# Agent attention with a cosine feed-forward layer: the running maximum and sum of the keys made on GpSimd from copies in SBUF

## The chip, the cores and the metric

The kernel runs on one core of one Trainium2 chip. The metric is the device time of one execution in microseconds (us), the median over repeated runs. A core has five engines with queues of their own: PE (TensorE, matmuls; PEld is its weight load), DVE (VectorE), ACT (ScalarE), POOL (GpSimd) and SP (SyncE, which here only issues DMAs).

## What is computed

Four batches of 12480 queries, keys and values of width 128, with 49 agents per batch, go through agent attention; its output goes through a layer of 2048 hidden units whose activation is h·cos(h).

```python
def sm(a, b):
    s = scale * (a @ b.transpose(0, 2, 1))
    s = s - s.max(-1, keepdims=True)
    e = np.exp(s)
    return e / (e.sum(-1, keepdims=True) + 1e-09)
agent_v = sm(agents, k) @ v          # agents over all keys
x = sm(q, agents) @ agent_v          # queries over the 49 agents
h = x @ w_in
out = (h * np.cos(h)) @ w_out
```

## The kernel before

Names: batch b is 0 to 3; NG = 13 groups of 960 queries per batch; a group is worked in STEP = 16 steps, and a batch in PER = 208 steps. One **step** of the main loop (first_product, cubic_part, second_product) is: two matmuls of 480 columns into a tile `ph` (L1063), a Sin activation on ACT that reads `ph` and writes `c` (L1066), one SCALAR_TENSOR_TENSOR on DVE that makes r = (c - 1)·h from `c` in SBUF and `ph` in PSUM (L1072), and, four steps later, two matmuls of `r` (L1088). There are 832 steps, and three `ph` tiles, so PE can be at most three steps ahead of DVE. Every eight steps two more matmuls end an output chunk (L1084, L1085), and ACT copies it to SBUF (L1095).

Everything else is fitted between the steps of the batch before it, by a table of step numbers (`plan`, `extra`, `spread_out`, `burst`, `fill`). For batch b = 1 to 3 that is, in the steps of batch b - 1:

- **The scores of the keys** (`Later.scores`, g = 0 to 12, NL = 13): 64 small matmuls (L552) into a PSUM tile `one`, of which there are two; ACT copies it to `s` in SBUF (L556; for g = 0 to 2 of batch 1 DVE copies). For g > 0 DVE takes the running maximum `run` = max(`run`, scores) at L559, elementwise, 128x392 elements (96x98 for g = 12), from PSUM, or from `s` where DVE copied. The scores of a query group (L169, copy L689, row maximum L693 on DVE, subtraction L695 on POOL) lie between them.
- **The maximum** over all keys: `top` (L566), two small matmuls (L570, L578), and `shift`: POOL subtracts it from the thirteen parts of `s` (L584).
- **A burst** at step 97 of the batch: the exponentials of `s` (L587) and of two pieces of queries (L746).
- **The sums**: POOL adds the parts of exp(s) into `es` (L593, at steps 44 + 3g behind the burst) and sums each query's 49 weights by a tree of additions (`query_sum`, L757 to L761). `query_inverse` adds EPS = 1e-9 on DVE (L765) and takes the reciprocal (L766), over a whole piece of 5 to 7 groups. `inverse` first calls `total`, which reduces `es` on DVE (L611), copies the result (L612), and is followed by a matmul with ones (L617).
- **The values**: matmuls L516 and a DVE addition into `av` (L606).
- **The weights of the queries**: for each group POOL multiplies (L771) into one of two tiles `p`, PE transposes it six steps before the group's first step (L785), ACT copies (L790), and POOL splits the copy into a rounded part and a rest, `pT` (two CASTs L795, two subtractions L796). The products L1063 of the group read `pT`.

The order on an engine is that of a scheduler; what stands inside `kept_behind` is held behind what the named engine was given before it, and all that `plan` runs is so held on DVE. In the windows around the bursts the order on PE, DVE and ACT is as written.

Of the kernel before, what the change touches and what calls it, by code (L numbers as in the profile page):

```python
# [9 lines left out]
F32 = mybir.dt.float32  # L10
# [4 lines left out]
ALU = mybir.AluOpType  # L15
AX = mybir.AxisListType
PSUM = bass.MemoryType.PSUM

P = 128
# [9 lines left out]
EPS = 1e-9  # L29
# [9 lines left out]
HI = 64  # L39
# [7 lines left out]
def agent_attention_cos_ffn(ctx, tc, qT, kT, v, vk, vk_rest, agT, w_in, w_out, outT):  # L47
    nc = tc.nc
    NB, _, N = qT.shape
    NA = agT.shape[2]  # L50
    KR = HI + NA
# [204 lines left out]
    class Agents:  # L256
# [88 lines left out]
        def total(self):  # L345

            self.es2 = self.sb.tile([TT, KR], F32, name="es2", bufs=1)
            nc.gpsimd.memset(self.es2, 0.0)
            nc.vector.tensor_reduce(self.es2[:, :NA], self.es.rearrange("p t a -> p a t"), axis=AX.X, op=ALU.add)
            nc.vector.tensor_copy(self.es2[:, HI:], self.es2[:, :NA])  # L350
# [54 lines left out]
    NL = -(-N // FULL)  # L405
# [129 lines left out]
    class Later(First):  # L535

        def scores(self, g, by_vector=False):
            sb = self.sb
            if g == 0:
                self.s = sb.tile([P, NT_K, NA], F32, name="s", bufs=1)  # L540
                self.run = sb.tile([P, 8, NA], F32, name="run", bufs=1)
                self.es = sb.tile([P, 8, NA], F32, name="es", bufs=1)
                nc.gpsimd.memset(self.s[REST:, 8 * (NL - 1):], -1e30)
            n = min(FULL, N - g * FULL)
            xt = sb.tile([P, 2 * 512], F32, name="xt", bufs=3)[:, :n]
            load(xt, kT[self.b, :, g * FULL:g * FULL + n])
            s = self.part(g)
            w, k, _ = s.shape
            ps = self.psum()[:w, :k * NA].rearrange("p (t a) -> p t a", a=NA)
            for t in range(k):  # L550
                for j in range(w // QS):
                    mm = nc.tensor.matmul(ps[j * QS:(j + 1) * QS, t], xt[:, t * w + j * QS:t * w + (j + 1) * QS],  # L552
                                          ag[:, self.b, :], start=True, stop=True)
                    if t == j == 0:
                        behind(mm)
            (nc.vector.tensor_copy if by_vector else nc.scalar.copy)(s, ps)  # L556
            if g > 0:
                run = self.run[:w, :k]
                nc.vector.tensor_max(run, self.part(0) if g == 1 else run, s if by_vector else ps)  # L559

        def part(self, g):
            return self.s[:, 8 * g:8 * g + 8] if g + 1 < NL else self.s[:REST, 8 * g:]
# [43 lines left out]
                nc.vector.tensor_add(self.av[:, :NA], self.av[:, :NA], po)  # L606

        def total(self):
            self.es2 = self.sb.tile([P, KR], F32, name="es2", bufs=1)
            nc.gpsimd.memset(self.es2[:, NA:HI], 0.0)  # L610
            nc.vector.tensor_reduce(self.es2[:, :NA], self.es.rearrange("p t a -> p a t"), axis=AX.X, op=ALU.add)  # L611
            nc.vector.tensor_copy(self.es2[:, HI:], self.es2[:, :NA])  # L612

        def inverse(self):
            self.total()
            pa = self.psum()
            nc.tensor.matmul(pa[:KR, :1], self.es2, ones, start=True, stop=True)  # L617
            self.rz = self.sb.tile([KR, 1], F32, name="rz", bufs=1)
            nc.vector.tensor_scalar_add(self.rz, pa[:KR, :1], EPS)
            nc.vector.reciprocal(self.rz, self.rz)  # L620
# [14 lines left out]
    with ExitStack() as pools:  # L635
# [27 lines left out]
        PER = NG * STEP  # L663
        NQ = NB * NG
        NSTEP = NB * PER
        e_of, rz_of = {}, {}
        PIECES = 7

        def piece_tiles(piece):
            e = sb.tile([QT, PIECES * GT, NA], F32, name="e", bufs=3)  # L670
            rz = sb.tile([QT, PIECES * GT], F32, name="rz2", bufs=4)
            for i, k in enumerate(piece):
                e_of[k], rz_of[k] = e[:, i * GT:(i + 1) * GT], rz[:, i * GT:(i + 1) * GT]
                e_of[piece], rz_of[piece] = e[:, :len(piece) * GT], rz[:, :len(piece) * GT]

        def query_parts(n, piece, wide=False, by_vector=False):
            b, g = n // NG, n % NG
# [73 lines left out]
        def query_sum(n):  # L751

            e, rz = e_of[n], rz_of[n].unsqueeze(2)
            t = sb.tile([e.shape[0], GT, 24], F32, name="tree", bufs=1)
            src, w = e, 24
            while w > 2:
                nc.gpsimd.tensor_add(t[:, :, :w], src[:, :, :w], src[:, :, w:2 * w])  # L757
                src, w = t, w // 2
            nc.gpsimd.tensor_add(rz, t[:, :, 0:1], t[:, :, 1:2])
            nc.gpsimd.tensor_add(rz, rz, t[:, :, 2:3])  # L760
            nc.gpsimd.tensor_add(rz, rz, e[:, :, 48:49])  # L761

        def query_inverse(piece):
            rz = rz_of[piece]
            nc.vector.tensor_scalar_add(rz, rz, EPS)  # L765
            nc.vector.reciprocal(rz, rz)  # L766

        def query_weights(n):
# [226 lines left out]
        for b in range(1, NB):  # L995
            o, ps = (b - 1) * PER, pieces[b - 1]
            at = o + BURST
            qs = [x for piece in ps for x in scored(piece)][ahead:]
            ks = [(ab[b].scores, g) for g in range(3 if b == 1 else 0, NG)]
            before = sum(1 for x in qs) - AFTER  # L1000
            t = spread_out(mixed(ks, qs[:before]), t, at - TURN, True)
            t = extra(t, ab[b].across, dense=True)
            plan(t - 1, ab[b].top)
            t = extra(t + 1, ab[b].spread, dense=True) + 1
            for g in range(NL):
                plan(t + g, ab[b].shift, g)
            t = spread_out(qs[before:], t, at - 5, True)
            assert t < at, (t, at)
            work = dict(A=(query_exp, ps[0]), B=(query_exp, ps[1]), K=(pinned_exp, ab[b]))
            burst(at, [work[x] for x in ('A', 'K', 'B')])  # L1010
            fresh = scored(pieces[b][0], False, True)
            ahead = len(fresh)
            vs = [(ab[b].values, g) for g in range(NG)]
            judged(at)
            fill(at, fresh, vs)
            fresh = [x[:3] for x in fresh]
            for g in range(1, NL):
                plan(at + 44 + 3 * g, ab[b].add, g)
            t, end = at + 5, o + PER - 26
            todo = mixed(vs, fresh)  # L1020
            for i, x in enumerate(todo):
                t = extra(t, *x, dense=True) + 1
                if i + 1 < len(todo):
                    t += max(0, (end - t) // (len(todo) - i - 1) - 1)
            t = extra(t, ab[b].folded) + 1
            t = extra(t, ab[b].inverse) + 1
            i = b % 2
            for c in range(DFF // 512):
                t = extra(t, ab[b].project, c, a[i], dense=True) + 1
            t = extra(t, ab[b].project_out, wio, b1[i], b2[i], dense=True)  # L1030
            later.append((ab[b], a[i]))
            t += 1
            assert t < o + PER + 4, (t, o + PER)
# [256 lines left out]
```

## Time and profile before

| | |
|---|---|
| median of 3 runs | 1098.57 us (1098.48 to 1100.44) |
| the profiled execution's own time | 1100.26 us |
| its span, first to last instruction | 1098.5 us |
| what lies around the span | 1.8 us |
| PE busy | 1044.0 us (95%) |
| DVE busy | 1027.6 us (94%) |
| ACT busy | 954.1 us (87%) |
| POOL busy | 460.5 us (42%) |
| mean granted TensorE clock | 0.984 of full speed |

The profile is of one execution. Busy time is the time in which an engine had an instruction under way; matmuls are pipelined and their ends are modelled, so a busy PE is not PE at its peak. The waits name, for each idle stretch of an engine, the instruction whose end released it. The chain is followed back from the last instruction, at each step to what released it. L559 is line 559 of the kernel before; the changed file has other line numbers (L1072 becomes L1093).

### The profile page before, as it was taken

The page shows a single profiled execution, that of the slowest core. Times are in us where ns is not written, and L with a number is a line of the kernel's source. Part 1 is how long each engine was busy: PE and PEld are TensorE (multiplying, and loading weights), DVE is VectorE, ACT ScalarE, POOL GpSimd, SP SyncE. Part 2 cuts the span into 40 slices and gives each one's busy share as a digit, 9 for nine tenths or more (in the row PEclk, how much of TensorE's full clock was granted, in tenths as well). Part 3 has the DMA queues.
Part 4 walks back from the last instruction along what each step waited for, and adds up shares of the span by engine and source line. Part 5 has one row for each costly group of instructions (what it writes and reads, how often), then busy time and mean ns, then how long its engine had stood idle before and what let it go on. Part 6 is the DMA issues. An engine that isn't in the chain of part 4 may idle for free.

```text
span 1098.5 us, 28945 instructions
## 1 busy us (share of the span) xinstructions
PE 1044.0 (95%) x12029; PEld 797.2 (73%) x12029; DVE 1027.6 (94%) x1139; ACT 954.1 (87%) x1196; POOL 460.5 (42%) x761
## 2 busy tenths in 40 slices
PE   6888999799999999989999999989999999989997
PEld 2766777687877787677786788767776777767775
DVE  6879999699999999989998999979998999999997
ACT  4678888898989999899888999888888999999996
POOL 2432326784522223786543131678362312252220
PEclk9899999899999999999999999989999999989999
DMA  9933566522002245442111234441100000000001
GB/s 357 339 92 115 150 188 226 168 83 90 23 36 95 77 131 175 137 157 79 44 54 58 93 95 164 140 151 58 60 20 37 18 36 19 37 18 36 19 37 40
DMA packets 32557, 108.49 MB, mean 99 GB/s; under 512 B 3616, under 2 KB 4896, under 8 KB 32416
## 3 DMA queue, kind: packets, MB, share of 16 engines
q1 hardware_dynamic: 32416, 106.55, 29.0%
q8 instruction: 97, 1.59, 0.6%
q14 instruction: 44, 0.36, 0.1%
HBM read 80.97 MB, written 25.56 MB: 97 GB/s over the span
## 4 chain that ended last, share of the span: by engine, by line
PE 52%; DVE 29%; ACT 7%; POOL 6%; issue 4%; DMA 1%; SPq 0%; ACTq 0%; POOLq 0%; DVEq 0%
DVE r L1072 26%; PE ph L1063 21%; PE one L1088 18%; ACT c L1066 4%; POOL s L584 3%; PE one L516 3%; PE one L169 2%; PE one L1084 1%; PE one L552 1%; PE one L1085 1%; PE one L785 1%; ACT s L587 1%; PE one L373 1%; DVE run L559 1%; ACT osb L1095 1%
## 5 line engine op out<-in xcount | busy, mean ns | idle before, releaser
L1072 DVE SCALAR_TENSOR_TENSOR r<-c,ph 128x960 fp32r<-128x960 f32 x832 | 909.4, 1147 | 31.3 <-ACT c L1066 29.3
L1066 ACT ACTIVATE c<-ph 128x960 f32<-128x960 f32 x832 | 790.2, 979 | 99.4 <-PE ph L1063 75.7
L1063 PE MATMUL ph<-pT,a 113*128 113x480 f32 x1664 | 537.2, 403 | 18.2 <-DVE r L1072 11.8
L1088 PE MATMUL one<-r,w 128*128 128x480 f32 x1664 | 503.6, 389 | 0.4 <-DVE r L1072 0.4
L1063 PEld LDWEIGHTS ph<-pT,a 113*128 113x128 f32 x1664 | 287.7, 190 | 141.3 <-DVE r L1072 76.2
L1088 PEld LDWEIGHTS one<-r,w 128*128 128x128 f32 x1664 | 309.1, 190 | 50.8 <-DVE r L1072 1.4
L771 POOL TENSOR_TENSOR p<-e,rz 126x392 f32<-126x392 f32 (+1 forms) x52 | 44.2, 851 | 314.1 <-PE one L785 300.3
L796 POOL TENSOR_TENSOR pT<-p,pT 49x480 fp32r<-49x480 f32 x104 | 126.9, 1220 | 7.9
L795 POOL CAST pT<-p 49x480 fp32r<-49x480 f32 x104 | 60.7, 584 | 61.9 <-ACT p L790 57.5
L695 POOL TENSOR_TENSOR e<-e,mx 126x392 f32<-126x392 f32 x43 | 36.2, 842 | 90.4 <-DVE mx L693 90.0
L757 POOL TENSOR_TENSOR tree<-tree 126x96 f32<-126x96 f32 (+1 forms) x141 | 43.8, 311 | 10.6
L1095 ACT COPY osb<-one 128x480 f32<-128x480 f32 x80 | 44.5, 556 | 3.9 <-PE one L1088 3.9
L516 PEld LDWEIGHTS one<-s,vt 128*32 128x32 f32 (+1 forms) x2352 | 31.1, 115 | 22.6 <-issue 13.7
L516 PE MATMUL one<-s,vt 128*32 128x49 f32 (+1 forms) x2352 | 37.3, 216 | 10.2 <-ACT s L587 7.0
L169 PEld LDWEIGHTS one<-ag,xt 128*32 128x32 f32 (+1 forms) x2752 | 32.9, 109 | 17.4 <-issue 14.4
L169 PE MATMUL one<-ag,xt 128*32 128x49 f32 (+1 forms) x2752 | 39.1, 209 | 2.9 <-issue 2.9
L584 POOL TENSOR_TENSOR s<-s,mxb 128x392 f32<-128x392 f32 (+1 forms) x39 | 34.3, 911 | 17.1 <-DVE mxb L580 17.1
L1084 PE MATMUL one<-pT,b 113*128 113x480 f32 x104 | 40.5, 389 | 0.0
L1085 PE MATMUL one<-pT,b 113*128 113x480 f32 x104 | 40.0, 385 | 0.0
L552 PEld LDWEIGHTS one<-ag,xt 128*32 128x32 f32 x2340 | 28.3, 110 | 15.1 <-issue 7.7
L552 PE MATMUL one<-ag,xt 128*32 128x49 f32 x2340 | 33.6, 209 | 2.0 <-DVE s L556 2.0
L757 POOL TENSOR_TENSOR tree<-e 126x192 f32<-126x192 f32 (+1 forms) x47 | 28.9, 615 | 11.2 <-ACT e L746 8.9
(151 smaller groups left out, 654.9 us busy)
## 6 DMA issues: line engine op xcount, KB each, us to landing
xt<-qT SPq DMA_DIRECT2D x51, 480.0 KB, 4.0
outT<-osb SPq DMA_DIRECT2D x51, 480.0 KB, 2.7
xt<-kT SPq DMA_DIRECT2D x42, 512.0 KB, 3.8
vt<-vk SPq DMA_DIRECT2D x36, 512.0 KB, 4.5
c<-kT SPq DMA_DIRECT2D x6, 512.0 KB, 6.1
c<-vk SPq DMA_DIRECT2D x6, 512.0 KB, 7.4
xt<-vk SPq DMA_DIRECT2D x6, 512.0 KB, 7.6
vt<-w_in SPq DMA_DIRECT2D x8, 256.0 KB, 6.4
```

What stands on the lines that cost most here:

```text
L169: mm = nc.tensor.matmul(out[at:at + n], xt[:, t * TT + lo:t * TT + lo + n], ag, start=True, stop=True)
L516: mm = nc.tensor.matmul(po[rows], vt[:, x, rows], e, start=(first and x == 0), stop=(last and x + 1 == len(es)))
L552: mm = nc.tensor.matmul(ps[j * QS:(j + 1) * QS, t], xt[:, t * w + j * QS:t * w + (j + 1) * QS], ag[:, self.b, :], start=True, stop=True)
L584: nc.gpsimd.tensor_sub(s, s, self.mxb.unsqueeze(1).to_broadcast(list(s.shape)))
L757: nc.gpsimd.tensor_add(t[:, :, :w], src[:, :, :w], src[:, :, w:2 * w])
L795: nc.gpsimd.tensor_copy(pT[own, c], p[own])
L796: nc.gpsimd.tensor_sub(pT[other, c], p[own], pT[own, c].bitcast(F32))
L1063: nc.tensor.matmul(ph[:, j, :CH], ai[:, f], pTs[q % 3][:, c], start=True, stop=True)
L1066: nc.scalar.activation(cos, h, AF.Sin, bias=HALF_PI, scale=1.0)
L1072: nc.vector.scalar_tensor_tensor(r, cos, 1.0, h, op0=ALU.subtract, op1=ALU.mult)
L1088: nc.tensor.matmul(po, w1[:, f, :], r[:, j, :], start=(f == 0), stop=(f == NF - 1))
L1095: nc.scalar.copy(osb[:, c * CH:(c + 1) * CH], po)
```

## The change

For g = 1 to 10 of each of the batches 1 to 3 the running maximum is no longer one DVE instruction but three on POOL (`larger`): the difference y - x into a tile `over`, its maximum with 0, and x plus that; y is the copy `s` in SBUF. For g = 11 and 12 DVE takes the maximum, always from PSUM. `total` is made on POOL, by additions that halve `es` three times, and is planned 83 steps behind the burst, no longer called by `inverse`. The constant EPS of a piece of queries is added on POOL behind the sum of the piece's last group, for all pieces but the `early` one and the first three groups of the kernel.

```diff
@@ Later.scores
             if g > 0:
                 run = self.run[:w, :k]
-                nc.vector.tensor_max(run, self.part(0) if g == 1 else run, s if by_vector else ps)
+                old = self.part(0) if g == 1 else run
+                if g < NL - 2:
+                    self.larger(run, old, s)
+                else:
+                    nc.vector.tensor_max(run, old, ps)
+
+        def larger(self, out, x, y):
+
+            over = self.sb.tile([P, 8, NA], F32, name="over", bufs=1)
+            with kept_behind([nc.gpsimd.engine]):
+                nc.gpsimd.tensor_sub(over, y, x)
+                nc.gpsimd.tensor_scalar(over, over, 0.0, None, op0=ALU.max)
+                nc.gpsimd.tensor_add(out, x, over)
@@ Later.total, inverse
         def total(self):
+            es = self.es
             self.es2 = self.sb.tile([P, KR], F32, name="es2", bufs=1)
-            nc.gpsimd.memset(self.es2[:, NA:HI], 0.0)
-            nc.vector.tensor_reduce(self.es2[:, :NA], self.es.rearrange("p t a -> p a t"), axis=AX.X, op=ALU.add)
-            nc.vector.tensor_copy(self.es2[:, HI:], self.es2[:, :NA])
+            with kept_behind([nc.gpsimd.engine]):
+                nc.gpsimd.memset(self.es2[:, NA:HI], 0.0)
+                for n in (4, 2):
+                    nc.gpsimd.tensor_add(es[:, :n], es[:, :n], es[:, n:2 * n])
+                for x in (slice(0, NA), slice(HI, KR)):
+                    nc.gpsimd.tensor_add(self.es2[:, x], es[:, 0], es[:, 1])
 
         def inverse(self):
-            self.total()
@@ piece_tiles
+            if piece != early:
+                closes[piece[-1]] = piece
@@ query_sum, query_inverse
             nc.gpsimd.tensor_add(rz, rz, e[:, :, 48:49])
+            if n in closes:
+                nc.gpsimd.tensor_scalar_add(rz_of[closes[n]], rz_of[closes[n]], EPS)
 
         def query_inverse(piece):
             rz = rz_of[piece]
-            nc.vector.tensor_scalar_add(rz, rz, EPS)
+            if piece not in closes.values():
+                nc.vector.tensor_scalar_add(rz, rz, EPS)
             nc.vector.reciprocal(rz, rz)
@@ the plan of batch b
             for g in range(1, NL):
                 plan(at + 44 + 3 * g, ab[b].add, g)
+            plan(at + 44 + 3 * NL, ab[b].total)
```

How the instructions move, at three places. First DVE, where the keys of batch 2 are scored (`run` is the running maximum, `mx` the row maximum of a query group, `r<-c,ph` the steps). Before:

```order
L693 TENSOR_REDUCE mx_5004<-e 126x8
L1072 SCALAR_TENSOR_TENSOR r<-c,ph 128x960 x8
L559 TENSOR_TENSOR run<-s,one 128x392
L1072 SCALAR_TENSOR_TENSOR r<-c,ph 128x960 x8
L559 TENSOR_TENSOR run<-run,one 128x392
```

and in the change:

```order
L710 TENSOR_REDUCE mx_5036<-e 126x8
L1093 SCALAR_TENSOR_TENSOR r<-c,ph 128x960 x36
L710 TENSOR_REDUCE mx_5603<-e 126x8
L1093 SCALAR_TENSOR_TENSOR r<-c,ph 128x960 x28
L710 TENSOR_REDUCE mx_6098<-e 126x8
L1093 SCALAR_TENSOR_TENSOR r<-c,ph 128x960 x10
L563 TENSOR_TENSOR run<-run,one 128x392
```

The maxima between the steps are gone up to the eleventh, which stays on DVE.

Second POOL at the same place (`p` is the weights of a query group, `pT` its split copy). Before:

```order
L695 TENSOR_TENSOR e<-e,mx_5004 126x392
L771 TENSOR_TENSOR p_104<-e,rz_2366 126x2x4x49
L795 CAST pT_100<-p 49x480 x2
L796 TENSOR_TENSOR pT_100<-p,pT_100 49x480 x2
L771 TENSOR_TENSOR p_105<-e,rz_2366 126x2x4x49
L795 CAST pT_98<-p 49x480 x2
```

and in the change:

```order
L712 TENSOR_TENSOR e<-e,mx_5036 126x392
L569 TENSOR_TENSOR over<-s 128x392
L570 TENSOR_SCALAR over<-over 128x392
L571 TENSOR_TENSOR run<-s,over 128x392
L791 TENSOR_TENSOR p_104<-e,rz_2396 126x2x4x49
L815 CAST pT_100<-p 49x480 x2
L816 TENSOR_TENSOR pT_100<-p,pT_100 49x480 x2
L569 TENSOR_TENSOR over<-s,run 128x392
L570 TENSOR_SCALAR over<-over 128x392
L571 TENSOR_TENSOR run<-run,over 128x392
```

The three instructions stand between one group's `pT` and the next group's `p`, not between a `p` and its `pT`.

Third POOL in the denser scores of batch 1, where it is otherwise at one place. In the change:

```order
L569 TENSOR_TENSOR over<-s,run 128x392
L570 TENSOR_SCALAR over<-over 128x392
L791 TENSOR_TENSOR p_104<-e,rz_751 126x2x4x49
L571 TENSOR_TENSOR run<-run,over 128x392
L815 CAST pT_99<-p 49x480 x2
L816 TENSOR_TENSOR pT_99<-p,pT_99 49x480 x2
```

Here the last of the three comes between the weights `p` and the split copy `pT`.

## Rows read from the trace of the kernel before

**Rows 1.** The page's first part: busy us (share of the span) and instructions of each engine.
```profile
PE 1044.0 (95%) x12029; PEld 797.2 (73%) x12029; DVE 1027.6 (94%) x1139; ACT 954.1 (87%) x1196; POOL 460.5 (42%) x761
```
**Rows 2.** The page's chain that ended last, by line.
```profile
DVE r L1072 26%; PE ph L1063 21%; PE one L1088 18%; ACT c L1066 4%; POOL s L584 3%; PE one L516 3%; PE one L169 2%; PE one L1084 1%; PE one L552 1%; PE one L1085 1%; PE one L785 1%; ACT s L587 1%; PE one L373 1%; DVE run L559 1%; ACT osb L1095 1%
```
**Rows 3.** Busy time by stretch: length, each engine's busy us, clock, DMA share, GB/s.
```profile
105.00:175.00 70.00, 69.67 (x1460) 55.07 (x1458) 67.94 (x80) 60.43 (x81) 24.41 (x29) 1.00 0.58 177
345.00:387.00 42.00, 41.60 (x484) 32.34 (x484) 41.45 (x42) 38.25 (x49) 9.75 (x11) 1.00 0.27 86
387.00:436.00 49.00, 48.88 (x714) 39.46 (x713) 48.37 (x50) 44.85 (x59) 14.03 (x16) 1.00 0.44 139
...
180.00:250.00 70.00, 64.18 (x1056) 51.03 (x1056) 60.47 (x69) 62.01 (x67) 57.23 (x123) 0.95 0.40 129
850.00:950.00 100.00, 99.18 (x423) 72.87 (x421) 99.64 (x95) 94.26 (x120) 26.74 (x30) 1.00 0.06 25
```
**Rows 4.** The chain in order of time: start us, us on the chain, what.
```profile
99.09 0.57 DVE run L559
...
262.31 0.77 DVE rz L765
...
321.18 0.76 DVE es L611
...
657.74 0.47 DVE run L559
```
**Rows 5.** Groups by line and shape: count, busy us, mean ns, idle before, releasers.
```profile
L1072 DVE SCALAR_TENSOR_TENSOR r<-c,ph 128x960 fp32r<-128x960 f32 x832 | 909.4, 1147 | 31.3 <-ACT c L1066 29.3
L1063 PEld LDWEIGHTS ph<-pT,a 113*128 113x128 f32 x1664 | 287.7, 190 | 141.3 <-DVE r L1072 76.2 <-issue 17.6 <-POOL pT L796 3.1
L559 DVE TENSOR_TENSOR run<-run,one 128x392 f32<-128x392 f32 x29 | 16.0, 553 | 0.0
L765 DVE TENSOR_SCALAR rz<-rz 126x48 f32<-126x48 f32 x3 | 2.6, 858 | 0.0
L611 DVE TENSOR_REDUCE es<-es 128x49 f32<-128x392 f32 x3 | 2.5, 843 | 0.0
L765 DVE TENSOR_SCALAR rz<-rz 126x56 f32<-126x56 f32 x3 | 0.8, 263 | 0.0
```
**Rows 6.** Waits, 345 to 387 us: engine line <- releaser: us, times, longest.
```profile
PEld ph L1063 <- DVE r L1072: 3.3, 9, 0.5
```
**Rows 7.** Waits, 387 to 436 us.
```profile
PEld ph L1063 <- DVE r L1072: 0.8, 2, 0.5
```
**Rows 8.** Waits, 105 to 152 us.
```profile
PEld ph L1063 <- DVE r L1072: 1.0, 2, 0.7
```
**Rows 9.** Waits, 310 to 335 us.
```profile
PEld ph L1063 <- DVE r L1072: 2.5, 4, 1.0
```
**Rows 10.** Groups of POOL by line and shape, columns as in rows 5.
```profile
L593 POOL TENSOR_TENSOR es<-es,s 128x392 f32<-128x392 f32 x30 | 31.1, 1037 | 2.2
L376 POOL TENSOR_SCALAR a<-a 113x512 fp32r<-113x512 f32 x14 | 8.6, 613 | 22.1 <-ACT a L374 22.1
```
**Rows 11.** Waits over the whole span.
```profile
POOL p L771 <- PE one L785: 300.3, 36, 14.0
```
**Rows 12.** Timeline, 259 to 266 us: start us, us, engine, line, operation.
```profile
260.52 2.51 POOL L796 TENSOR_TENSOR pT<-p,pT 49x480 fp32r<-49x480 f32 x2
262.23 0.85 DVE L765 TENSOR_SCALAR rz<-rz 126x48 f32<-126x48 f32 x1
```
**Rows 13.** Busy time of L1072 alone in one stretch: length, DVE busy us.
```profile
180.00:250.00 70.00, 53.68 (x50) 0.95 0.40 129
```
**Rows 14.** Timeline, 345 to 375 us: a group's transposes and the end of its split.
```profile
354.53 0.60 PE L785 MATMUL one<-ident,p 126*113 126x126 f32 x4
...
357.52 2.51 POOL L796 TENSOR_TENSOR pT<-p,pT 49x480 fp32r<-49x480 f32 x2
```
**Rows 15.** Busy time of L559 alone in one stretch, columns as in rows 13.
```profile
387.00:436.00 49.00, 3.87 (x7) 1.00 0.44 139
```

More of the change, by code (lines that the diff above doesn't have):

```diff
@@ L665, in agent_attention_cos_ffn @@
         NSTEP = NB * PER
-        e_of, rz_of = {}, {}
+        e_of, rz_of, closes = {}, {}, {}
         PIECES = 7
```

## The prediction

> **What bounds the kernel now.** I read the busy shares first: PE 95%, DVE 94%, ACT 87%, POOL 42% [rows 1]. Two engines are nearly full, so what DVE gains only counts where PE waits for DVE. The chain says the same [rows 2]: the step's DVE instruction L1072 has 26%, the two step matmuls of PE 21% and 18%, so the end is set by PE and DVE in turns. The reader is to see next which of them it is in the stretches that the change touches [rows 3]. Where the keys are scored (105 to 175, 345 to 387, 387 to 436 us; batch 3 repeats batch 2 some 260 us later) DVE is busy 97 to 99% and PE 99%, which overstates PE. PE's own waits are the better measure: over the whole span its weight loads of the first product waited 76.2 us for L1072, the end of which frees a `ph` tile, and only 3.1 us for `pT` from POOL [rows 5]. By stretch those waits for DVE are 3.3 us in 345 to 387 [rows 6], 0.8 in 387 to 436 [rows 7], 1.0 in 105 to 152 [rows 8], and 2.5 at the end of batch 1's sums, 310 to 335 [rows 9]. ACT is the third: 91% in 345 to 387, against the 94% that it reaches in 850 to 950, where no scores are made and DVE is busy 99.6% [rows 3]. That 94% I take as what ACT can carry beside a full DVE.
>
> **What leaves DVE.** (1) Thirty running maxima: 28 of 0.553 us, and two from SBUF that I price alike; 16.6 us. (2) Three times the reduction of `es`, 0.843 [rows 5]; 2.5 us (the copy behind it is small and left out). (3) Seven additions of EPS: three of 0.858, three of 0.263 [rows 5], and a shorter one priced at 0.26; 3.6 us. Together 22.7 us of DVE, the ceiling of the gain.
>
> **How much of it lies on the path.** On the chain in order of time sixteen of the moved maxima appear, from 99.09 to 657.74 us: the two of the burst at 0.57 each, fourteen at 0.47; with them all three reductions (first at 321.18, 0.76) and the three longer EPS additions (first at 262.31, 0.77) [rows 4]. That is 7.7 + 2.3 + 2.3 = 12.3 us, if nothing else becomes late in their place. What is late next, stage by stage:
>
> - 345 to 387 and its twin in batch 3, four maxima each: DVE gives back 4 x 0.47 = 1.9, and PE waits 3.3, so PE allows it. ACT's 38.25 us at 94.3% need 40.6 of the 42 us, so 1.4 is what I take. Twice: 2.8.
> - 387 to 436 and its twin, six maxima each: DVE would give 2.8, but PE waits for it only 0.8, since score blocks follow each other here twice as closely. Twice 0.8: 1.6.
> - 105 to 175, eight maxima: 3.8 on DVE, PE waits 1.0; I take 1.0.
> - The burst at 99 us, where DVE makes copies, sums and maxima in a row: 2 x 0.57 = 1.1.
> - Reductions 2.3 (PE waits 2.5 there, so it is paid in full) and EPS 2.3. The shorter EPS additions are not on the chain: 0.
>
> The EPS additions are long for a reason that the timeline shows: the one at 262.23 ends at 263.08, just when POOL's L796, begun at 260.52, ends [rows 12]; the wider ones beside no such instruction took 0.263 [rows 5]. The reciprocal behind it then starts from what POOL wrote; POOL's own addition stands behind the last sum, long before the reciprocal's step, so I price it at 0, at most 0.6 (L376's row) each.
>
> **What POOL gets.** Thirty times a subtraction, a maximum with 0 and an addition: nearest rows 1.037 us for an addition of this shape and 0.613 for a two-operation TENSOR_SCALAR of 512 columns [rows 10], scaled to 392 some 0.5; 2.6 in all, 78 us. Three totals of at most 1.04 + 1.04 + 2 x 0.6, and seven EPS additions under 0.6: 14 at most. POOL goes from 460 to at most 552 us, 50%. The cover is its idle time: in 345 to 387 it is busy 9.75 of 42 us, and four maxima add 10.4; over the span it stood 300.3 us waiting for PE's transposes before the next `p` [rows 11]. In batch 1 cover is thin: 24.41 of 70 us plus eight times 2.6 is 65%, in lumps. Queued behind the new instructions are the `pT` splits, for which PE waits. In 345 to 375 the transposes begin at 354.3, the half of `pT` that is needed first is done when the first of two subtractions, half of 2.51 us, ends at 358.8 [rows 14], and the group begins six steps behind the transposes; at 1.14 us a step (in 345 to 387 us DVE has 42 instructions, of which four are maxima and one a row maximum [rows 3]) that is 361.1. So `pT` has 2.3 us to spare, about one whole running maximum. The order of the change puts none between a `p` and its `pT`, but for one addition of 1.04 in batch 1. Between 0 and 1.04 I take 1.0 for lateness there, since PE sets the pace in that stretch.
>
> DVE now waits for POOL at the eleventh maximum, and the steps queue behind it. In 387 to 436 us seven maxima lie some 7 us apart [rows 15], against 2.6 of POOL each, so I price this wait at 0, with 1 us for each batch as its upper end.
>
> A rule speaks against the move. The row: one DVE maximum is 0.553 us, what replaces it 2.6. The Trainium skill (GPSIMD Engine Reference, 4.1 Engine selection) gives elementwise adds and maxima to VectorE, GpSimd being about 2x slower with two inputs; the rows agree, 1.037 against 0.553. By it alone, if POOL were the path, the sum would be thirty times 2.05 us slower.
>
> **The sum.** 2.8 + 1.6 + 1.0 + 1.1 + 2.3 + 2.3 - 1.0 = 10.1 us. From the profiled execution's 1100.26 that is 1090.2; this execution stands 1.7 us above the median of the runs, 1098.57, and from the median I predict **1088.5**.
>
> **The rivals.**
> - *The bound just passes to PE and ACT.* For it: in the scores PE is busy 99%, and it waits for DVE only 0.8 and 1.0 us in two of the three kinds of stretch. Against it: 3.3 and 2.5 us in the others. Then little but the EPS additions remains, some 3 us: 1095.5.
> - *All of DVE's time comes out*, because PE's busy share is modelled and its waits are understated: up to 22.7 us, 1076. Against it: ACT's 91%.
> - *POOL becomes late (slower).* Place: the `pT` splits of the fourteen groups in the score stretches, queued behind running maxima. It decides once POOL runs more than the 2.3 us behind; two maxima in a row, 5.2 us, would stall PE 2.9 at each group, 41 us against 11 gained: 1129; at half of the groups 1108. Against it: the order, and 3.1 us of waits for `pT` so far.
> - *POOL's reads hold up DVE (slower).* The EPS row shows that one kind of DVE instruction waits for POOL. If L1072 did, ninety new POOL instructions of 0.87 us would each cost half their length, 39 us, less 11: 1127. Against it: with POOL busy 82%, 180 to 250 us, L1072 took 53.68 / 50 = 1.07 us [rows 13]; where POOL is busy 27%, DVE's 95 instructions took 1.05 each [rows 3]. The Trainium skill (SBUF — State Buffer, Who interferes with whom) says that a DVE instruction with two SBUF inputs, or in a two-port mode, shares a port with GpSimd and blocks, and that one with a single SBUF input does not. By that rule L1072, which reads `ph` from PSUM, is free; the trace agrees, 1.07 against 1.05, and also for the EPS addition, 0.858 against 0.263.
> - *It doesn't do what it says*: the order shows the maxima gone from DVE, so this is left out.
>
> **How the numbers follow.** Something under 0.2%, 2.2 us, is no change to a measurement of this kernel. Forecast (5 to 15 us saved) 0.68; bound passes on (0 to 5) 0.16, a third of it under 2.2 us; all of it (over 15) 0.07; POOL late 0.06; port 0.03. Faster: 0.68 + 0.07 + 0.10 = 0.85; same 0.06 plus 0.02 for a POOL that gives back just what is gained: 0.08; slower 0.07. The range takes the forecast and most of the bound that passes on, 1081.5 to 1097, leaving out the two slower cases and the ends.
>
> **What would show it.** Right: DVE some 20 us less busy, PE's weight loads waiting 5 us or more less for L1072, POOL near 545 us, batch 2's and 3's scores 2 us shorter each, the ends of the sums 0.8. Wrong: waits of L1084 (the changed file's first product) for `pT` well above 3.1 us, DVE idle before the eleventh maximum, or the score stretches as long as before with ACT or PE at their shares.

## The result, and the profile after

The change takes 1088.55 us (median of 4 runs, 1087.31 to 1089.89) against 1099.30 before on the same chip (4 runs, 1098.48 to 1100.44): a ratio of 0.9894, 95% interval [0.9878, 0.9909]. The forecast was 1088.5 us. A second series of the same kernel on another chip, 1089.69 (1088.65 to 1089.88) against 1100.77, gives 0.9899 [0.9883, 0.9914]. The profiled execution of the change took 1087.5 us, with a span of 1085.7; it is compared below with the profiled one of before, 1100.26, so these two differ by 12.8 us, 2 us more than the medians do. In the changed file the step's DVE instruction L1072 is L1093, the first product L1063 is L1084, the second L1088 is L1109, and the maximum on POOL is L569, L570 and L571.

The page's first part after the change, against [rows 1]:

```profile
PE 1035.9 (95%) x12029; PEld 800.6 (74%) x12029; DVE 1011.0 (93%) x1096; ACT 952.6 (88%) x1196; POOL 564.5 (52%) x870
```

DVE has 43 instructions fewer and is busy 16.6 us less; POOL has 109 more and is busy 104 us more. DVE's records lie partly over each other, so its busy time falls by less than the durations of what left: 832 steps of mean 1149 ns would be 956 us, and their row below says 909.2.

The chain of work that ended last, by engine and then by line, against [rows 2]:

```profile
PE 61%; DVE 21%; ACT 7%; POOL 6%; issue 3%; DMA 1%; SPq 0%; ACTq 0%; POOLq 0%; DVEq 0%
PE ph L1084 25%; PE one L1109 22%; DVE r L1093 20%; ACT c L1087 3%; PE one L516 3%; PE one L552 2%; POOL s L596 2%; PE one L169 2%; PE one L1105 2%; PE one L1106 1%; POOL tree L774 1%; PE one L805 1%; PE one L373 1%; ACT s L599 1%; PE ph L494 1%
```

The step on DVE goes from 26% to 20%, and PE's two step matmuls from 39% to 47%. None of the three POOL lines of a maximum is among the fifteen. With 104 us more of POOL's work its share of the chain is still 6%.

Waits over the whole span, of PE's weight loads and products at the step's first matmul and of POOL before the next `p`, against [rows 5, 11] (engine, line, what it waited for: us, times, longest):

```profile
POOL p L791 <- PE one L805: 186.9, 28, 12.8
...
PEld ph L1084 <- DVE r L1093: 58.6, 178, 4.2
...
PE ph L1084 <- DVE r L1093: 7.0, 12, 3.8
...
PEld ph L1084 <- POOL pT L816: 3.6, 4, 1.2
```

PE's weight loads wait 17.6 us less for DVE. They wait for `pT` 3.6 us where it was 3.1. POOL's own idle time before the next `p` fell from 300.3 to 186.9 us: this is where the new work went.

Busy time in the stretches of [rows 3], cut at the same steps of the main loop, so that a shorter stretch is time saved (length, then each engine's busy us, clock, DMA share, GB/s):

```profile
103.30:172.98 69.68, 69.43 (x1459) 55.45 (x1459) 64.52 (x72) 59.72 (x81) 51.76 (x55) 1.00 0.57 176
339.47:379.76 40.29, 40.29 (x485) 32.97 (x484) 39.88 (x38) 38.21 (x49) 22.84 (x23) 1.00 0.29 91
379.76:428.51 48.75, 48.46 (x712) 39.53 (x711) 46.32 (x44) 44.42 (x59) 33.75 (x34) 1.00 0.44 140
```

The middle row is what was 345 to 387 us. It went from 42.00 to 40.29 us; PE is now busy in all of it and ACT at 38.21 / 40.29 = 95%, with DVE at 99%: three engines full at once. The first and the last row give back only 0.32 and 0.25 us. In batch 1's scores POOL went from 35% to 74%.

Groups by line and shape, columns as in [rows 5]:

```profile
L1093 DVE SCALAR_TENSOR_TENSOR r<-c,ph 128x960 fp32r<-128x960 f32 x832 | 909.2, 1149 | 36.3 <-ACT c L1087 32.9
L570 POOL TENSOR_SCALAR over<-over 128x392 f32<-128x392 f32 x30 | 35.6, 1188 | 2.6
L571 POOL TENSOR_TENSOR run<-run,over 128x392 f32<-128x392 f32 x27 | 28.1, 1043 | 2.2
L569 POOL TENSOR_TENSOR over<-s,run 128x392 f32<-128x392 f32 x27 | 28.0, 1038 | 33.8 <-ACT s L556 33.6
L563 DVE TENSOR_TENSOR run<-run,one 128x392 f32<-128x392 f32 x3 | 1.7, 559 | 0.1
L786 DVE RECIPROCAL rz<-rz 126x48 f32<-126x48 f32 x3 | 1.3, 445 | 0.0
L780 POOL TENSOR_SCALAR rz<-rz 126x56 f32<-126x56 f32 x3 | 1.1, 353 | 0.3
L780 POOL TENSOR_SCALAR rz<-rz 126x40 f32<-126x40 f32 x1 | 0.3, 313 | 0.1
```

The step is 1149 ns as before (1147), the eleventh maximum L563 waits 0.1 us, and a maximum on POOL is 1038 + 1188 + 1043 ns, 3.27 us.

**A ledger by steps.** The Sin activation of every step is in the trace, so its start dates the step in any of the kernels. The table gives us between the starts of two steps, for one profiled execution of each kernel (the runs are told below; "total + EPS" is the change without its maxima):

| steps | what lies there | before | change | change again | maxima alone | total + EPS | total alone | EPS alone |
|---|---|---|---|---|---|---|---|---|
| 16 to 96 | scores, batch 1 | 109.7 | 108.2 | 108.1 | 108.2 | 109.9 | 109.8 | 109.6 |
| 96 to 112 | burst | 31.6 | 30.2 | 30.7 | 30.9 | 30.3 | 31.1 | 30.3 |
| 112 to 160 | an EPS addition | 55.0 | 54.1 | 54.2 | 55.1 | 54.2 | 55.1 | 54.3 |
| 160 to 208 | the total, batch 1 | 59.9 | 58.7 | 58.6 | 59.8 | 58.6 | 58.6 | 59.8 |
| 208 to 272 | scores, batch 2 | 74.2 | 72.2 | 72.2 | 72.2 | 74.2 | 74.2 | 74.2 |
| 304 to 336 | burst | 47.2 | 48.9 | 47.9 | 47.6 | 48.9 | 47.5 | 48.6 |
| 336 to 416 | EPS and total, batch 2 | 96.7 | 94.8 | 94.7 | 96.7 | 94.6 | 95.5 | 95.9 |
| 416 to 480 | scores, batch 3 | 74.2 | 72.2 | 72.2 | 72.3 | 74.2 | 74.2 | 74.3 |
| 512 to 544 | burst | 48.7 | 48.3 | 47.8 | 48.8 | 47.9 | 47.2 | 47.9 |
| 544 to 624 | EPS and total, batch 3 | 93.8 | 92.1 | 92.2 | 93.9 | 92.2 | 92.8 | 93.0 |

Steps 272 to 304 and 480 to 512 (40.4 to 41.5 us in all of these) and those behind 624 (227.7 to 228.9) are left out. Outside the bursts the kernels fall into two columns of numbers, with and without the part concerned, to 0.2 us. The bursts vary by more than that between executions of one kernel (the change twice: 48.9 and 47.9), which the last section takes up.

### The profile page after: what moved, and what is told of

Same layout as the page of the kernel before. It is cut to its first block, busy times and chain, and to the rows that moved or that the text cites. A ratio compares the mean times of both kernels' runs of the same rounds, so it can differ in the third digit from the quotient of the medians.

```text
span 1085.7 us, 29006 instructions
## 1 busy us (share of the span) xinstructions
PE 1035.9 (95%) x12029; PEld 800.6 (74%) x12029; DVE 1011.0 (93%) x1096; ACT 952.6 (88%) x1196; POOL 564.5 (52%) x870
## 4 chain that ended last, share of the span: by engine, by line
PE 61%; DVE 21%; ACT 7%; POOL 6%; issue 3%; DMA 1%; SPq 0%; ACTq 0%; POOLq 0%; DVEq 0%
PE ph L1084 25%; PE one L1109 22%; DVE r L1093 20%; ACT c L1087 3%; PE one L516 3%; PE one L552 2%; POOL s L596 2%; PE one L169 2%; PE one L1105 2%; PE one L1106 1%; POOL tree L774 1%; PE one L805 1%; PE one L373 1%; ACT s L599 1%; PE ph L494 1%
## 5 line engine op out<-in xcount | busy, mean ns | idle before, releaser
L1093 DVE SCALAR_TENSOR_TENSOR r<-c,ph 128x960 fp32r<-128x960 f32 x832 | 909.2, 1149 | 36.3 <-ACT c L1087 32.9
L1084 PE MATMUL ph<-pT,a 113*128 113x480 f32 x1664 | 532.9, 401 | 13.0 <-DVE r L1093 7.0
L1109 PE MATMUL one<-r,w 128*128 128x480 f32 x1664 | 505.8, 390 | 0.4 <-DVE r L1093 0.4
L1084 PEld LDWEIGHTS ph<-pT,a 113*128 113x128 f32 x1664 | 291.0, 190 | 124.1 <-DVE r L1093 58.6
L1109 PEld LDWEIGHTS one<-r,w 128*128 128x128 f32 x1664 | 309.0, 190 | 50.7 <-DVE r L1093 1.4
L791 POOL TENSOR_TENSOR p<-e,rz 126x392 f32<-126x392 f32 (+1 forms) x52 | 44.2, 851 | 194.8 <-PE one L805 186.9
L774 POOL TENSOR_TENSOR tree<-tree 126x96 f32<-126x96 f32 (+1 forms) x141 | 44.0, 312 | 10.6
L569 POOL TENSOR_TENSOR over<-s,run 128x392 f32<-128x392 f32 x27 | 28.0, 1038 | 33.8 <-ACT s L556 33.6
L169 PEld LDWEIGHTS one<-ag,xt 128*32 128x32 f32 x2752 | 32.9, 109 | 16.9 <-issue 11.9
L169 PE MATMUL one<-ag,xt 128*32 128x49 f32 x2752 | 39.1, 209 | 2.4 <-issue 2.4
L1105 PE MATMUL one<-pT,b 113*128 113x480 f32 x104 | 40.6, 390 | 0.0
L552 PEld LDWEIGHTS one<-ag,xt 128*32 128x32 f32 x2340 | 28.4, 110 | 15.9 <-issue 10.9
L570 POOL TENSOR_SCALAR over<-over 128x392 f32<-128x392 f32 x30 | 35.6, 1188 | 2.6
```

The costliest lines, as they stand in the source:

```text
L169: mm = nc.tensor.matmul(out[at:at + n], xt[:, t * TT + lo:t * TT + lo + n], ag, start=True, stop=True)
L1084: nc.tensor.matmul(ph[:, j, :CH], ai[:, f], pTs[q % 3][:, c], start=True, stop=True)
L1093: nc.vector.scalar_tensor_tensor(r, cos, 1.0, h, op0=ALU.subtract, op1=ALU.mult)
L1105: nc.tensor.matmul(po, b1[k], pTs[q % 3][:, c], start=False, stop=False)
L1109: nc.tensor.matmul(po, w1[:, f, :], r[:, j, :], start=(f == 0), stop=(f == NF - 1))
```

## The experiments

**The change again.** The same kernel, on another chip.

> The changed kernel once more, on the chip that runs the next three. Every theory expects the ratio measured already, 0.989, within 0.002; the runs of it so far lay in two heaps, near 1087.4 and 1089.7 us.

Measured: 1089.69 us, 0.9899 [0.9883, 0.9914]. The saving is there again.

**The maxima alone.** `total` and EPS are put back on DVE as before; the maxima stay on POOL.

```diff
-            plan(at + 44 + 3 * NL, ab[b].total)
...
         def inverse(self):
+            self.total()
...
-            if piece != early:
-                closes[piece[-1]] = piece
```

> Only the ten maxima per batch move to POOL; the reduction of es and the EPS additions are DVE's as before. The forecast's terms: 2.8 + 1.6 + 1.0 + 1.1 less 1.0 of lateness = 5.5 us saved against before, ratio 0.995. The rival that the bound just passes to PE and ACT: under 1.5 us saved, ratio 0.9985 or more. The EPS additions, back on DVE, are again as long as the POOL instruction beside them lets them be: 0.8 us where L796's like runs, under 0.35 elsewhere.

Measured: 1095.6 us, 0.9949 [0.9935, 0.9962], 5.2 us saved. By the ledger 1.5 + 2.0 + 1.9 us of it lie in the three batches' scores and nothing in the stretches of EPS and the totals. The EPS addition is again long on DVE. The group in this kernel:

```profile
L780 DVE TENSOR_SCALAR rz<-rz 126x48 f32<-126x48 f32 x3 | 2.6, 861 | 0.0
```

**The maxima undone.** `total` and EPS on POOL, the maxima on DVE.

```diff
-                if g < NL - 2:
-                    self.larger(run, old, s)
-                else:
-                    nc.vector.tensor_max(run, old, ps)
+                nc.vector.tensor_max(run, old, s if by_vector else ps)
```

> The maxima stay on DVE as before; the sums and EPS are POOL's as in the change. The forecast's terms: 2.3 + 2.3 = 4.6 us saved, ratio 0.996. The rival: nearly the whole 10.7 us of the change comes from here, ratio 0.990.

Measured: 1095.39 us, 0.9948 [0.9934, 0.9961], 5.4 us saved. With the 5.2 of the maxima alone this makes 10.6, against 10.8 to 11.1 for the change: the two halves add up, and neither takes the other's gain. The scores are as long as before (109.9, 74.2, 74.2), the stretches behind them as short as in the change.

**The total alone, and EPS alone.** The second half taken apart. In both the maxima are as in the kernel before; for the total alone, EPS goes back to DVE:

```diff
-            if piece != early:
-                closes[piece[-1]] = piece
```

and for EPS alone the total does:

```diff
-            plan(at + 44 + 3 * NL, ab[b].total)
...
         def inverse(self):
+            self.total()
```

> Only the reduction of es moves to POOL and into the plan; the maxima and EPS are as before. The forecast's term: 2.3 us saved, ratio 0.998; by the steps of the trace of the change, steps 160 to 208 of a batch and their like are 1 us shorter each. If the earlier matmul with ones is what pays, the saving lies before the projections (L373), if it is DVE's time, where L611 stood.

> Only the EPS of the seven pieces moves to POOL. The forecast's term: 2.3 us saved, ratio 0.998, 0.77 in each batch where the long addition stood. If the stall behind POOL's L796 just passes on to the reciprocal, it takes 0.8 us or more instead of 0.44 and nothing is saved.

Measured: the total alone 1097.58 us, 0.9959 [0.9943, 0.9974]; EPS alone 1098.95 us, 0.9991 [0.9976, 1.0006], which the times alone don't tell from no change. The ledger does: EPS alone is 0.7, 0.8 and 0.8 us shorter in the three stretches with a long EPS addition, 2.3 us in all, and the total alone 1.3, 1.2 and 1.0 us, 3.5 us. The interval of the total alone, 2.9 to 6.3 us, does not fix its size; its ledger does, with the same 1.2 us, to 0.1, in steps 160 to 208 in every kernel that has the total on POOL. Within them the saving lies between steps 188 and 204, where the reduction, its copy and the matmul with ones all stand, so the place doesn't say which of them pays.

**No maxima for g = 1 to 10,** so that POOL's new work is gone and DVE's is as in the change.

```diff
-                if g < NL - 2:
-                    self.larger(run, old, s)
-                else:
-                    nc.vector.tensor_max(run, old, ps)
+                if g >= NL - 2:
+                    nc.vector.tensor_max(run, self.part(0) if g == NL - 2 else run, ps)
```

> Left out: the maxima over parts 1 to 10 of the keys, on either engine, so that the shift is the maximum over three of the thirteen parts; the rest as in the change. POOL loses 30 x 3.3 = 98 us of work, DVE's work is that of the change. If lateness on POOL costs what I took, it is 1.0 us faster than the change, all of it in batch 1's scores; if POOL's maxima are wholly hidden, the same within 0.5 us; if POOL's reads hold up DVE's step instruction, many us faster and L1072's like shorter than the 1149 ns of the change.

Measured: 1088.76 us, 0.9888 [0.9872, 0.9903], which is the change's: 0.9 us less than the change on the same chip (1089.69), less than the interval, so the times alone don't decide between the first two cases of the expectation. The page's first part and the step's group in this kernel:

```profile
PE 1036.6 (95%) x12029; PEld 800.9 (74%) x12029; DVE 1010.8 (93%) x1096; ACT 952.9 (88%) x1196; POOL 468.4 (43%) x780
```

```profile
L1090 DVE SCALAR_TENSOR_TENSOR r<-c,ph 128x960 fp32r<-128x960 f32 x832 | 909.0, 1149 | 35.8 <-ACT c L1084 31.9
```

With 96 us of POOL's work gone, the step on DVE is 1149 ns as with it, and by steps the scores are as long as in the change, 108.1, 72.2 and 72.2 us, so nothing was lost to lateness there. So in the change the thirty maxima cost nothing that the runs can show: POOL is neither late nor in DVE's way.

**Every maximum twice on POOL.** The first of the two goes to a spare tile, so only POOL's work grows.

```diff
-                nc.gpsimd.tensor_sub(over, y, x)
-                nc.gpsimd.tensor_scalar(over, over, 0.0, None, op0=ALU.max)
-                nc.gpsimd.tensor_add(out, x, over)
+                for into in (self.sb.tile([P, 8, NA], F32, name="spare", bufs=1), out):
+                    nc.gpsimd.tensor_sub(over, y, x)
+                    nc.gpsimd.tensor_scalar(over, over, 0.0, None, op0=ALU.max)
+                    nc.gpsimd.tensor_add(into, x, over)
```

> Every running maximum on POOL is made twice, the first time into a spare tile, so POOL gets 30 x 3.3 = 98 us more, and each maximum takes 6.6 us; the output is that of the change. In batch 1's scores (105 to 175 us) POOL's work becomes 24.4 + 8 x 6.6 = 77 of 70 us: it no longer fits, so pT comes late there and, by the rival of a late POOL, at some of the later groups too, where two lie in a row: 2.9 us and more at each. If POOL's cover is as I said (idle for most of batches 2 and 3), only batch 1 pays, 7 us or so, up to 15: ratio against before 0.996 to 1.004. If POOL is never on the path, 0.990 as the change.

Measured: 1146.21 us, 1.0412 [1.039, 1.0433]. The expectation missed by far: some 57 us above the change, for 96 us more of POOL's busy time (660.9 us), and not in batch 1 alone. Against the change steps 16 to 96 are 24.6 us longer (132.8), 208 to 272 9.6 (81.8), and 272 to 304 6.4 (47.0 against 40.6); the twins in batch 3 are 9.6 and 6.7 longer. Its waits over the whole span:

```profile
PEld ph L1085 <- POOL pT L817: 30.6, 16, 7.2
PE ph L1085 <- POOL pT L817: 24.3, 11, 6.8
...
DVE run L563 <- POOL run L572: 12.4, 3, 5.1
```

This is the rival "POOL becomes late", made to happen: the weight loads' waits for `pT`, 3.6 us in the change, are 30.6, the products' 24.3, and the eleventh maximum waits 12.4. The step on DVE is not what got longer. With POOL busy 660.9 us it still takes its 1149 ns:

```profile
L1094 DVE SCALAR_TENSOR_TENSOR r<-c,ph 128x960 fp32r<-128x960 f32 x832 | 911.2, 1149 | 78.9 <-ACT c L1088 75.6
```

Two stretches of this kernel's chain in order of time, at 111 and at 400 us (L570 to L572 are its maxima):

```profile
111.03 1.02 POOL over L570
112.05 0.52 POOL pT L816
112.58 1.17 POOL over L571
...
113.82 1.20 POOL pT L817
...
115.06 0.70 PE ph L1085 x2
...
400.04 1.22 POOL pT L817
401.32 1.23 POOL pT L817
402.62 1.04 POOL over L570
403.73 1.20 POOL over L571
```

In batch 1 a `pT` split lies behind the maxima, PE's next product behind that. Behind 400 us the chain runs on POOL from one maximum to the next. The windows of this kernel over batch 1's scores and the denser scores of batch 2:

```profile
104.00:202.00 98.00, 82.59 (x1475) 64.58 (x1473) 69.29 (x76) 63.77 (x86) 87.09 (x88) 0.88 0.42 132
402.00:467.00 65.00, 53.72 (x769) 43.22 (x768) 47.85 (x46) 46.55 (x60) 58.07 (x58) 0.92 0.36 113
```

POOL is busy 89% in both, and has become the pace; a good part of the rest is gaps of some 0.08 us between its instructions. That could be seen ahead, and the expectation had seen it for batch 1: the change has 51.76 us of POOL in 69.68, and eight times 3.27 more is 77.9, more than the stretch holds. The same count for the denser half of batch 2, 33.75 and six times 3.27, is 53.4 us of 48.75, which the expectation passed over when it took POOL for idle there. The price was wrong too: the counts are 8.2 and 4.6 us over, and steps 16 to 96 are 24.6 us longer, 208 to 304 16.0. Why lateness costs that much more than the work that doesn't fit was not taken apart; the granted clock of these windows is 0.88 and 0.92, where the change has 1.00.

**The same with slower maxima.** The doubled form again, with the maximum with 0 in a form of two operations, which was meant to be the faster one.

```diff
-                    nc.gpsimd.tensor_scalar(over, over, 0.0, None, op0=ALU.max)
+                    nc.gpsimd.tensor_scalar(over, over, 0.0, 3e38, op0=ALU.max, op1=ALU.min)
```

> Every maximum on POOL made twice, but with the two-operation form: if that is the fast one, 5.2 us for each where the doubled kernel had 6.6 and the change 3.3. The doubled kernel lost 57 us to the change, which I put down to POOL's queue running behind in the score stretches, where its work exceeds the time: 24 + 8 x 6.6 = 77 of 70 us in batch 1, 14 + 6 x 6.6 = 54 of 49 in the close blocks of batches 2 and 3. With 5.2 it is 66 of 70 and 45 of 49: by that account most of the 57 us go, and 0 to 20 remain. If it was instead that any second maximum in a row comes between a p and its pT, whatever the sum, 40 us or more remain.

Measured: 1166.17 us, 1.0600 [1.058, 1.0619]. The premise fell, since two operations take longer than one (next experiment), so the run can't decide between the two cases of its expectation, which hang on a faster form. It gives a slope, though. In this kernel:

```profile
L571 POOL TENSOR_SCALAR over<-over 128x392 f32<-128x392 f32 x60 | 91.1, 1518 | 5.0
```

Its 60 instructions are 0.33 us longer each, 20 us, and the kernel is 20.0 us slower than the doubled one above (1166.17 - 1146.21; the kernel before was 1.0 us faster on this one's chip). Here, where POOL sets the pace in the scores, what it is given comes out in the time about one for one; in the change, where it does not, the 96 us of its maxima came out at zero.

**What the maximum with 0 costs.** It was priced at 0.5 us and takes 1.19. Two causes were tried: the second operation that the row used for the price has, and the tile's shape of three dimensions. Two operations:

```diff
-                nc.gpsimd.tensor_scalar(over, over, 0.0, None, op0=ALU.max)
+                nc.gpsimd.tensor_scalar(over, over, 0.0, 3e38, op0=ALU.max, op1=ALU.min)
```

and the flat form:

```diff
-                nc.gpsimd.tensor_scalar(over, over, 0.0, None, op0=ALU.max)
+                flat = over.rearrange("p t a -> p (t a)")
+                nc.gpsimd.tensor_scalar(flat, flat, 0.0, None, op0=ALU.max)
```

> The maximum with 0 on POOL is written with two operations (maximum with 0, minimum with 3e38), as L376's TENSOR_SCALAR has two; the output is that of the change. I had priced this instruction at 0.5 us from L376's row (613 ns for 512 columns), and it took 1188 ns. If the form with one operation is the slow one, it falls to some 0.5 us and POOL loses 30 x 0.7 = 21 us; if the shape or the maximum is, it stays at 1.19. The time is that of the change within 1 us either way, since leaving POOL's maxima out altogether gave 0.9 us.

> The same instruction with one operation, but on a view of 392 columns in place of 8 x 49. If the two-level shape makes it slow, 0.5 us; else 1.19.

Measured: 1088.82 us, 0.9901 [0.9885, 0.9917] with two operations; 1087.52 in a single run of the flat form. The rows, of the one and of the other:

```profile
L570 POOL TENSOR_SCALAR over<-over 128x392 f32<-128x392 f32 x30 | 45.6, 1519 | 2.6
```

```profile
L570 POOL TENSOR_SCALAR over<-over 128x392 f32<-128x392 f32 x30 | 35.7, 1190 | 2.6
```

Two operations are slower, 1519 ns, so the expectation of some 0.5 us missed; the shape changes nothing. Why L376 does two operations on 512 columns in 0.613 us [rows 10] stays open: its output type, its 113 partitions and its constants (a minimum first, then a maximum) differ, and none of these was tried. The time of the kernel doesn't move, as it shouldn't with POOL hidden.

**Eleven maxima on POOL,** with one operation and with two.

```diff
-                if g < NL - 2:
+                if g < NL - 1:
```

> The eleventh maximum moves to POOL as well, so that DVE keeps only the last, small one. DVE loses 3 x 0.56 us more. If POOL keeps up, up to 1.4 us faster than the change, ratio against before 0.988 to 0.989; if the last maximum on DVE then waits for POOL, the steps behind it on DVE stand, DVE shows an idle stretch before L563, and it is up to 3 us slower than the change, 0.992.

> Two operations as in the run before, and the eleventh maximum on POOL too. If the eleventh paid nothing because POOL's 3.3 us made the last maximum wait, the shorter 2.6 us lets it pay, up to 1.4 us against the change; if PE sets the pace there, as its waits for DVE of 0.8 us in 387 to 436 us of the trace of before say, the same as the change.

Measured: 1088.69 us, 0.9893 [0.9874, 0.9911], and 1090.22 us, 0.9905 [0.9888, 0.9922]. Both are the change's time within the intervals. The last maximum, L563, has 0.0 us idle before it in both, so it does not wait for POOL; another 0.56 us less of DVE per batch just gives nothing that can be measured, in a stretch where PE's weight loads waited only 0.5 us for DVE in the change. Of all kernels that were run, none beats the change by more than its interval.

## Why the prediction held, step by step

The mechanism was the one forecast. That the time agrees to 0.05 us is luck: the forecast was counted from 1098.57 us, 0.73 below the median of before that the change is compared with, and the sum was 0.65 too small. The sum, 10.1 us, stands against 1099.30 - 1088.55 = 10.75 of the medians; the terms as the ledger has them make 1.5 + 4.0 + 2.3 + 3.5 = 11.3. What the two profiled executions differ by beyond that, 12.8 - 11.3, lies ahead of the first step, in the bursts and behind step 624. Term by term, some came out smaller and some larger than forecast:

- *Scores of batches 2 and 3*, 2.8 + 1.6 = 4.4 forecast. Measured 2.0 for each batch, 4.0. The limit was set from PE's waits and from ACT's share, and these are what now hold the stretch: PE busy 40.29 of 40.29, ACT at 95% where 94.3% had been taken as the most it can carry, and the wait for DVE down from 3.3 [rows 6] to 1.0 us. In the denser half 0.8 us had been read from [rows 7], and 0.5 of waiting is left. By halves the forecast is less good than by batches: 1.4 became 1.7, and the 0.8 of the denser half became 0.25. The waits of [rows 6, 7] in this change:

```profile
PEld ph L1084 <- DVE r L1093: 1.0, 4, 0.3
...
PEld ph L1084 <- DVE r L1093: 0.5, 2, 0.2
```

- *Batch 1's scores with the two long maxima at 99 us*, 1.0 + 1.1 = 2.1 forecast, less 1.0 for lateness. Measured 1.5: 1.2 of it in steps 24 to 28, where the two long maxima stood, and 0.3 in the stretch of the eight others, for which 1.0 had been taken from PE's wait [rows 8]. There was no lateness, since the kernel without any maxima on POOL is just as long there (108.1). The place where an addition comes between `p` and its `pT` shows why. The timeline of POOL in the change (start us, us):

```profile
145.95 0.84 POOL L791 TENSOR_TENSOR p<-e,rz 126x392 f32<-126x392 f32 x1
146.76 1.05 POOL L571 TENSOR_TENSOR run<-run,over 128x392 f32<-128x392 f32 x1
147.77 1.22 POOL L815 CAST pT<-p 49x480 fp32r<-49x480 f32 x2
149.06 2.52 POOL L816 TENSOR_TENSOR pT<-p,pT 49x480 fp32r<-49x480 f32 x2
```

  This `pT` is that of the group whose transposes began at 143.87 us, so its cast comes 3.90 us behind them. In the kernel before the cast at 150.80 came 1.46 behind transposes at 149.34. It is 2.4 us later, then, and still PE has no wait for `pT` between 140 and 156 us: the transposes run six steps ahead of the group, and a step takes 1.36 us here (69.68 us for 51.4 steps), not the 1.14 that the spare of 2.3 us was worked out from; six times the difference make it 3.6. So two terms of this stretch were off, the gain of the eight maxima by 0.7 us and the lateness by 1.0, with opposite signs; that they nearly cancel is luck.
- *EPS*, 2.3 forecast, 2.3 measured in the run that moves it alone. The reciprocal behind it is not held up by POOL: 445 ns, 0.0 idle.
- *The totals*, 2.3 forecast, 3.5 measured: the term that was under-sized. The reduction is 0.76 us on the chain [rows 4], but the copy behind it (L612), which was left out as small, lay in the same queue. Three times 0.843 and three copies of 0.181 make 3.1; that the copy makes up the difference is worked out from these durations, and no run moves it alone. In the change the matmul with ones also stands earlier. Timeline rows of before and of the change:

```profile
323.37 0.27 PE L617 MATMUL one<-ones,es 128*113 128x1 f32 x2
```

```profile
313.92 0.33 PE L632 MATMUL one<-ones,es 128*113 128x1 f32 x2
```

  By the steps it stands at step 192.7 before and at 188.2 in the change, so PE meets it, and what it releases, four steps earlier; that may be the remaining 0.4 us, but no run separates this.
- *POOL's work* was put at 2.6 us for a maximum and is 3.27, since the maximum with 0 was priced from L376's row; POOL is busy 564.5 us and not at most 552. Nothing hangs on it here: with 74% in batch 1's scores there was still room. The EPS rows, had they existed, would have given the price: from 40 to 56 columns they go from 313 to 353 ns, 2.5 ns a column, so 353 + 336 x 2.5 = 1193 ns at 392, an estimate that L570's 1188 bears out. The Trainium skill (GPSIMD Engine Reference, 4.1 Engine selection) has only GpSimd's operations with two inputs at half of VectorE's rate and says that "1-input is roughly line-rate". The rows bear it out in part: L376, with one input and 512 columns, takes 613 ns on POOL [rows 10] and 418 in the one place where the kernel before has it on DVE; but the maximum with 0, with one input, takes 1188 ns, more than the 1038 of two inputs.

Of the rivals, *the bound just passes to PE and ACT* is in part what happened in the scores, where the maxima had 7.7 us on the chain and brought 5.5; but the rival had left them next to nothing, and the totals were paid in full besides. *All of DVE's time comes out* fell at the same place: the maxima that left DVE there come to 16.6 us. *POOL's reads hold up DVE* fell with the step at 1147, 1149 and 1149 ns (before, change, no maxima). The 1.07 and 1.05 us that the prediction set against this rival are not of one kind, since the first is busy time of L1072 alone and the second that of all DVE instructions; by their own durations the L1072 of the two stretches take 1146 and 1148 ns, which says the same. *POOL becomes late* did not happen, but its price was of the right order: doubling POOL's part brings it out, with 57 us where the rival had 41 for `pT` alone.

## To carry to other kernels

When work leaves a nearly full engine, read stage by stage how long the next engine waits for it, and cap the gain there by that wait and by the third engine's share; do this before adding up durations, which here were twice the gain. In these runs the wait was an upper bound: where it was 3.3 us the stretch gave back 1.7, where it was 1.0 and 0.8 only about 0.3 each. On the engine that takes the work, add its new busy time to the old in the densest stretch, not over the span: 52% of the span was 74% there, free, and twice the work did not fit: it cost 57 us, and from there on each us more of it was about a us of time. What lies in the same queue behind the moved instruction, a small copy too, belongs to the sum.

## What was not expected of the hardware

TENSOR_SCALAR on POOL: 1188 ns for one operation on 392 columns, 1519 for two, against 613 ns for another form on 512 columns; above.

The bursts differ between executions by as much as a term of the sum, and in the change and in its other executions alike. Steps 304 to 336 took 47.2 us before, 48.9 in the change and 47.9 in its second profile. The granted clock is lowest in the longest. Windows over the first half of those steps (304 to 320), of before, of the change and of its second profile:

```profile
459.20:488.30 29.10, 24.85 (x584) 19.67 (x584) 24.47 (x32) 27.57 (x25) 22.21 (x59) 0.94 0.55 175
```

```profile
451.70:482.50 30.80, 25.94 (x585) 21.05 (x585) 24.32 (x32) 27.73 (x26) 23.69 (x61) 0.89 0.52 164
```

```profile
454.35:484.07 29.72, 25.12 (x584) 20.10 (x583) 24.62 (x33) 27.68 (x26) 22.69 (x60) 0.94 0.52 174
```

The chains of the three show where, in the same order. PE had waited for 4.20 us of exponentials on ACT in each, and the x35 is its first work behind them:

```profile
469.02 1.03 PE one L516 x35
...
473.47 0.44 PE one L1088 x2
```

```profile
461.52 0.63 PE one L516 x35
...
468.46 0.80 PE one L1109 x2
...
469.77 0.44 PE one L1109 x2
```

```profile
464.14 0.63 PE one L516 x35
...
470.14 0.44 PE one L1109 x2
```

Two matmuls of 480 columns take 0.80 us at the lower of the two clock levels, 1.2 GHz, and 0.44 at the upper, 2.4 GHz. The first pair at the upper level begins 4.45 us behind PE's first work in before, 8.25 in the change and 6.00 in its second profile. The 3.80 and 1.55 us more at half the speed are worth some 1.9 and 0.8 us, and the windows are 1.7 and 0.6 us longer. The last two are executions of the same kernel, so the change is not what sets this. Anyone who judges a term of 1 us from one profile has to leave such stretches out, as the ledger's other rows do.
